# Two dense products of a spectral stage issued as pairs of 64 output columns

## The chip, the cores and the metric

The kernel runs on one core of one Trainium2 chip. The metric is the device time in microseconds (us). A core has TensorE (PE, which multiplies matrices; the loading of its stationary operand is listed apart as PEld), VectorE (DVE), ScalarE (ACT), GpSimd (POOL) and SyncE (SP, which here issues DMAs). Each engine takes its instructions in the order of the program and waits for the others by semaphores.

## The reference

Two kinds of layer alternate, twice each, on one sequence of 2048 rows and 512 features. Layer A is a global filter in the frequency domain; layer B is a gated feed-forward layer without a nonlinearity.

```
def A(x, w_r, w_i):                 # x: 1 x 2048 x 512
    X = rfft2(x, axes=(-2, -1))
    return irfft2(X * (w_r + 1j * w_i), s=(2048, 512), axes=(-2, -1))

def B(x, w_gate, w_up, w_down):     # 512 -> 1792 -> 512
    return ((x @ w_gate) * (x @ w_up)) @ w_down

x = x + A(layernorm(x), A_w_r, A_w_i)
x = x + B(layernorm(x), B_w_gate, B_w_up, B_w_down)
x = x + A(layernorm(x), A_w_r, A_w_i)
x = x + B(layernorm(x), B_w_gate, B_w_up, B_w_down)
```

## The kernel before

The two-dimensional transforms are done as products with small constant matrices. A spectral layer has three stages. The forward stage takes the 16 row tiles of x one after the other (a product `tp` on TensorE each) and writes a spectrum `E`. The middle stage, which the change touches, works on 16 groups g of `E`. The inverse stage (`yi`, then `yo`) needs all 16 groups, and adds the result to `xs`, the residual stream. Then comes the feed-forward layer (`gx`, `gy`, `gw`, `gz`, `gv`, and `db` or `ex`, `ey`, `ew`, `ez`, `ev`), most of the run.

A group g goes through the middle stage in this way, one 128 x 512 tile in each step:

1. `fs`: sums and differences of halves of `E`, two instructions on POOL (on DVE for the first two groups).
2. `dp` (function `features` in `middles`): eight products of 64 output columns on PE. The stationary operand is 64 columns of `fs`, the moving one a 128 x 128 block of the constant `df`. They write partitions 0 to 63 and 64 to 127 of a PSUM bank in turn.
3. `zs`: ACT copies `dp` to SBUF.
4. `zp` (function `across` in `middle`): one product on PE with a constant 128 x 128 matrix from `midt` as the stationary operand, and all 512 columns of `zs` as the moving one. Group 0 has two products of 256 columns with two different matrices.
5. The complex filter `W` (tile `wq`), in one of two ways by turns. Way "1": ACT copies the two halves of `zp` into `jz`, DVE multiplies `zp`, POOL multiplies `jz`, DVE adds them to `ys`. Way "2": four instructions on DVE, which write `ys` and `qp`.
6. `vq` (function `back`): four products on PE with 128 x 128 blocks of `ys` as the stationary operand and a matrix from `midt` as the moving one.
7. `E`: ACT copies `vq` back into its place in `E`.

All products here are float32. Each is seen in the profile as two matmul records, its two passes, each with a weight load.

What stands where is not left to a scheduler: every step is recorded in a `Plan`, and a table of numbers, `ORDER`, gives the order in which the steps are issued; a second one, `PLACES`, gives each tile its buffer. Neither table is touched by the change. In this order PE takes several groups in turn, so that a `dp` of later groups stands between `zp` and `vq` of earlier ones. In each layer `dp` stands in 8 runs, of 24, six times 16, and 8 products. The product `wp`, which belongs to no result, is placed by the helper `idle` before the stage and after its last `vq`.

The kernel keeps eight banks of 128 x 512 in PSUM: `dp`, `zp` and `vq` take turns in those tagged x, a, d and w, and a product that writes a bank also waits for the last reader of what was in it.

Since a helper (line 314 in the profile) issues every recorded instruction, all rows of the profile carry that one line, and are told apart by the names of their tiles.

Of the kernel before, what the change touches and what calls it, by code (L numbers as in the profile page):

```python
# [283 lines left out]
def kernel(ctx: ExitStack, tc: tile.TileContext, x, wf, wc, wb, dfwd, tf, ti, mid, out):  # L284
# [8 lines left out]
    def bank(name, tag):  # L293
        t = Tile_(name, tag, lambda: pp.tile([128, 512], F32, name=name, tag=t.tag(), bufs=1))
        return t

    def temp(name, tag, shape=(128, 512), dt=F32):
        t = Tile_(name, tag, lambda: wk.tile(list(shape), dt, name=name, tag=t.tag(), bufs=1))
        return t
# [20 lines left out]
    V, A, G, TE, SP = (Queue(e) for e in (nc.vector, nc.scalar, nc.gpsimd, nc.tensor, nc.sync))  # L320
# [3 lines left out]
    def mm3(o, sh, sl, mh, ml, start, stop):  # L324
        for n, (a, b) in enumerate(((sh, mh), (sh, ml), (sl, mh))):
            TE.matmul(o, a, b, start=start and n == 0, stop=stop and n == 2, skip_group_check=True)

    def dve(n, fn, r, w, **kw):
        return plan.op("DVE", max(0.12, 0.07 + 0.00104 * n), 0.155 + 0.00104 * n, fn, r, w, **kw)

    def act(n, fn, r, w, more=0.0, **kw):
        return plan.op("ACT", 0.05 + 0.00086 * n + more, 0.16 + 0.00084 * n + more, fn, r, w, **kw)

    def pool(n, fn, r, w, **kw):
        return plan.op("POOL", 0.15 + 0.00215 * n, 0.2 + 0.0021 * n, fn, r, w, **kw)

    def pe(us, fn, r, w, **kw):
        return plan.op("PE", us, us, fn, r, w, **kw)
# [18 lines left out]
    f2, f20, g2, g20 = (midt[:, 128 * i:128 * i + 128] for i in range(4))  # L357
# [20 lines left out]
    def load_hp():  # L378
        load(32, lambda: SP.dma_start(hp, wc), (), ["hp"])
        dve(32, lambda: V.tensor_scalar(hp[:, 1], hp[:, 1], -1.0, None, op0=ALU.mult), ["hp"], ["hp"], due=HPDUE)  # L380
# [24 lines left out]
    def stats(t, nm, on_act=False):  # L405
        i = nm.ts.index(t)
        if on_act:
            z = temp("sq", "f")
            a = temp("ac", "st", (128, 6))
            act(512, lambda: A.activation(z(), xs[:, t], AF.Copy, accum_out=a()[:, 0:1]), [("xs", t)], [z, (a, 0)], more=0.25)  # L410
            act(20, lambda: A.mul(a()[:, 1:2], a()[:, 0:1], -1.0 / 512), [(a, 0)], [(a, 1)])
            act(512, lambda: A.activation(z(), xs[:, t], AF.Square, bias=a()[:, 1:2], accum_out=a()[:, 2:3]),
                [("xs", t), (a, 1)], [z, (a, 2)], more=0.25)
            dve(10, lambda: V.tensor_scalar(nm.mv()[:, i, 0:1], a()[:, 0:1], 1.0 / 512, None, op0=ALU.mult), [(a, 0)], [(nm.mv, i)])
            dve(10, lambda: V.tensor_scalar(nm.mv()[:, i, 1:2], a()[:, 2:3], 1.0 / 512, None, op0=ALU.mult), [(a, 2)], [(nm.mv, i)])
            return
        st = temp("st", "st", (128, 6))
        dve(512, lambda: V.bn_stats(st(), xs[:, t]), [("xs", t)], [st])
        dve(20, lambda: V.bn_aggr(nm.mv()[:, i], st()), [st], [(nm.mv, i)])
# [104 lines left out]
    def idle(n, key="idle", ring="w", cols=512):  # L524
        for i in range(n):
            bk = bank("wp", ring)
            pe(cols / 595, lambda bk=bk: TE.matmul(bk()[:, 0:cols], midt[:, 0:128], midt[:, 0:cols], start=True, stop=True), ["midt"], [bk, key])
# [29 lines left out]
    def middle(g, dp, E, W, due, swap):  # L557
        zs = temp("zs", "f")
        act(512, lambda: A.copy(zs(), dp()), [dp], [zs])
        zp = bank("zp", "da"[g % 2])  # L560

        def across():
            if g:
                TE.matmul(zp(), f2, zs(), start=True, stop=True)
            else:
                for q, m in enumerate((f20, f2)):
                    TE.matmul(zp()[:, 256 * q:256 * q + 256], m, zs()[:, 256 * q:256 * q + 256], start=True, stop=True, skip_group_check=True)

        pe(0.86, across, [zs, "midt"], [zp])
        y, w = temp("ys", "f"), W.key[g // 2]  # L570
        if swap == "1":
            jz = temp("jz", "f")
            act(512, lambda: A.mul(jz()[0:64], zp()[64:128], -1.0), [zp], [(jz, 0)], more=0.11)
            act(512, lambda: A.copy(jz()[64:128], zp()[0:64]), [zp], [(jz, 1)], more=0.11)
            dve(512, lambda: tt(zp(), zp(), W(g, 0), ALU.mult), [(jz, 0), (jz, 1), w], [zp])
            pool(512, lambda: gtt(jz(), jz(), W(g, 1), ALU.mult), [w], [(jz, 0), (jz, 1)])
            dve(512, lambda: tt(y(), zp(), jz(), ALU.add), [zp, (jz, 0), (jz, 1)], [y])
        else:
            qp = bank("qp", "y")
            dve(512, lambda: tt(y(), zp(), W(g, 0), ALU.mult), [zp, w], [y])  # L580
            dve(512, lambda: stt(qp()[0:64], zp()[64:128], -1.0, W(g, 1)[64:128], op0=ALU.mult, op1=ALU.mult), [zp, w], [(qp, 0)])
            dve(512, lambda: tt(qp()[64:128], zp()[0:64], W(g, 1)[0:64], ALU.mult), [zp, w], [(qp, 1)])
            dve(512, lambda: tt(y(), qp(), y(), ALU.add), [(qp, 0), (qp, 1)], [y])
        vq = bank("vq", "wd"[g % 2])

        def back():
            for q in range(2):
                for par in range(2):
                    o = 256 * q + 128 * par
                    TE.matmul(vq()[:, o:o + 128], y()[:, o:o + 128], g2 if g or q else g20, start=True, stop=True, skip_group_check=True)  # L590

        pe(0.92, back, [y, "midt"], [vq, *(["turn"] if g > 14 else [])])
        if g > 14:
            idle(1, "turn", "a")
        into = lambda: E()[:, :, :, g].rearrange("p b t (q e) -> p q (b t) e", q=2)
        act(512, lambda: A.copy(into(), vq().rearrange("p (q c e) -> p q c e", q=2, e=4)), [vq], [(E, "g", g, 0), (E, "g", g, 1)], more=0.11, due=due)
# [590 lines left out]
```

## Time and profile before

| | before |
|---|---|
| median of 3 runs | 1048.96 us (1048.85 to 1051.21) |
| profiled execution, first to last instruction (span) | 1048.2 us |
| instructions | 18805 |
| PE busy | 1032.4 us, 6560 matmul records |
| `dp` | 512 records of 128x128, stationary 128 x 64 |
| `zp` | 60 records of 128x512, 8 of 128x256, stationary 128 x 128 |
| `vq` | 256 records of 128x128, stationary 128 x 128 |
| granted PE clock | 1.000 |
| middle stage of layer 0 | 28.2 to 75.4 us of the span |
| middle stage of layer 1 | 548.1 to 594.0 us of the span |

The page has no other time of the profiled execution than its span; it is 0.8 us below the median. A row of the timeline reads: start and length in us, engine, line, operation, tile written and tiles read, for a matmul the array in use (`128*64` is 128 rows and 64 columns of the array), the shape, the number of merged records, and in square brackets how long the engine stood idle before it and which engine ended that. The ends of matmuls are modelled and rows of PE overlap, so the distance between two starts tells what a product costs, and not its length. Busy times of the engines overlap.

### The profile page before, as it was taken

Reading aid. Unit: us, or ns where it says so; the run is one execution under the profiler, and the core shown is the slowest. Engines: PE = TensorE matmul, PEld = TensorE weight load, DVE = VectorE, ACT = ScalarE, POOL = GpSimd, SP = SyncE. Lnnn points to the kernel's source line nnn. Section 1 sums busy time; section 2 is a strip of 40 time slices with the busy share of each in tenths; the row PEclk is TensorE's granted clock in tenths of the full one; section 3 lists DMA queues with packets and bytes.
Section 4 is the critical chain, followed back from the end, with each engine's and each line's share of the span. In section 5 each row is a group of like instructions: output and inputs, shape, how many; then the busy total and the mean of one; then the engine's idle time right before and its main releaser. Section 6 shows DMA issues by size and latency. Waiting matters only on the chain.

```text
span 1048.2 us, 18805 instructions
## 1 busy us (share of the span) xinstructions
PE 1032.4 (98%) x6560; PEld 900.8 (86%) x6560; DVE 803.6 (77%) x1581; ACT 421.0 (40%) x1011; POOL 747.0 (71%) x960
## 2 busy tenths in 40 slices
PE   9899999999999999999999999999999999999998
PEld 7677988888899888889987779888889998888887
DVE  7769867768877577878877697788888775767788
ACT  6568534343453232232366693223333421222231
POOL 6968899999999645566688367555578963536671
PEclk9999999999999999999999999999999999999999
DMA  9525266668773864646382005455787266464542
GB/s 360 224 83 191 64 218 229 234 214 277 253 213 140 278 215 158 201 164 230 120 319 78 6 12 201 153 176 176 190 275 219 91 222 220 162 211 179 213 141 81
DMA packets 129469, 193.66 MB, mean 185 GB/s; under 512 B 39264, under 2 KB 50784, under 8 KB 127328
## 3 DMA queue, kind: packets, MB, share of 16 engines
q1 hardware_dynamic: 129088, 191.95, 54.1%
q8 instruction: 52, 0.85, 0.3%
q10 hardware_dynamic: 288, 0.52, 0.1%
q14 instruction: 41, 0.34, 0.1%
HBM read 145.52 MB, written 46.92 MB: 184 GB/s over the span
## 4 chain that ended last, share of the span: by engine, by line
PE 90%; DVE 6%; POOL 1%; ACT 1%; DMA 1%; issue 1%; SPq 0%; DVEq 0%; POOLq 0%; ACTq 0%
PE gz L314 15%; PE gx L314 15%; PE db L314 8%; PE gy L314 7%; PE gw L314 7%; PE gv L314 7%; PE ex L314 5%; PE ez L314 5%; PE ey L314 3%; PE dp L314 3%; PE ev L314 3%; PE vq L314 3%; PE ew L314 3%; PE zp L314 2%; DVE xs L314 2%; PE yi L314 2%
## 5 line engine op out<-in xcount | busy, mean ns | idle before, releaser
L314 PE MATMUL gx<-xA,wt 128*128 128x512 f32 (+1 forms) x852 | 179.3, 346 | 0.0
L314 PEld LDWEIGHTS gx<-xA,wt 128*128 128x128 f32 x852 | 137.9, 190 | 17.9
L314 POOL TENSOR_TENSOR sf<-q,sf 128x256 fp32r<-128x256 f32 x99 | 73.0, 742 | 106.4 <-ACT sf L314 97.3
L314 POOL TENSOR_TENSOR sf<-cc,sf 128x256 fp32r<-128x256 f32 x97 | 71.7, 742 | 55.8 <-ACT sf L314 48.9
L314 DVE TENSOR_TENSOR xs<-xs,db 128x512 f32<-128x512 f32 x128 | 85.5, 681 | 23.1 <-PE db L314 22.6
L314 PE MATMUL db<-wd,h 128*128 128x512 f32 x336 | 91.1, 392 | 0.1
L314 PE MATMUL gy<-xS,wt 128*128 128x512 f32 (+1 forms) x426 | 89.9, 346 | 0.0
L314 PE MATMUL gz<-xS,wt 128*128 128x512 f32 (+1 forms) x426 | 89.9, 346 | 0.0
L314 PE MATMUL gz<-xA,wt 128*128 128x512 f32 (+1 forms) x426 | 89.6, 346 | 0.0
L314 PE MATMUL gw<-xS,wt 128*128 128x512 f32 (+1 forms) x426 | 89.5, 346 | 0.0
L314 PE MATMUL gv<-xS,wt 128*128 128x512 f32 (+1 forms) x426 | 89.4, 345 | 0.0
L314 ACT COPY s<-gx 128x512 f32<-128x512 f32 (+1 forms) x71 | 35.2, 496 | 132.0 <-PE gx L314 131.7
L314 PEld LDWEIGHTS gz<-xS,wt 128*128 128x128 f32 x426 | 69.0, 189 | 9.5 <-DVE q L314 0.4
L314 PEld LDWEIGHTS gw<-xS,wt 128*128 128x128 f32 x426 | 69.1, 189 | 9.1
L314 PEld LDWEIGHTS gz<-xA,wt 128*128 128x128 f32 x426 | 69.0, 189 | 9.0
L314 PEld LDWEIGHTS gv<-xS,wt 128*128 128x128 f32 x426 | 69.0, 190 | 9.0
L314 PEld LDWEIGHTS gy<-xS,wt 128*128 128x128 f32 x426 | 68.6, 190 | 8.6
L314 DVE TENSOR_TENSOR q<-gy,s 128x512 f32<-128x512 f32 (+1 forms) x71 | 41.0, 577 | 45.2 <-PE gy L314 33.0
L314 ACT CAST sf<-q 128x256 fp32r<-128x256 f32 x99 | 40.0, 407 | 82.0 <-DVE q L314 41.5
L314 PEld LDWEIGHTS db<-wd,h 128*128 128x128 f32 x336 | 61.1, 188 | 11.6 <-POOL h L314 0.2
L314 POOL TENSOR_TENSOR wt<-rg,wt 128x512 fp32r<-128x512 f32 (+1 forms) x56 | 64.2, 1158 | 5.2 <-ACT wt L314 5.1
L314 PE MATMUL ex<-bf,sf 128*128 128x256 f32 x396 | 58.1, 283 | 0.0
(166 smaller groups left out, 2507.9 us busy)
## 6 DMA issues: line engine op xcount, KB each, us to landing
wt<-gu SPq DMA_DIRECT2D x36, 1024.0 KB, 6.8
wt<-gu SPq DMA_DIRECT2D x36, 768.0 KB, 6.7
bf<-dn SPq DMA_DIRECT2D x20, 1024.0 KB, 5.4
wq<-in_wf_dram SPq DMA_DIRECT2D x16, 1024.0 KB, 8.3
bf<-dn SPq DMA_DIRECT2D x20, 768.0 KB, 4.7
gu<-wt SPq DMA_DIRECT2D x14, 1024.0 KB, 5.9
gu<-wt SPq DMA_DIRECT2D x14, 768.0 KB, 5.4
rg<-in_wb_dram SPq DMA_DIRECT2D x14, 512.0 KB, 3.9
```

Of the source, the lines that this page charges most:

```text
L314: ins = f(*args, **kw)
```

## The change

`zp` and `vq` are issued as pairs: a new helper `halves` takes columns 0 to 63 of the stationary operand into partitions 0 to 63 of the result, and then columns 64 to 127 into partitions 64 to 127, each with the whole moving operand. `dp` was issued in this form already. What is computed is the same. No step is moved, added or taken out, and no other engine has another instruction; only the numbers in the names of tiles differ.

```
+    def halves(o, a, b):
+        for c in (slice(0, 64), slice(64, 128)):
+            TE.matmul(o[c], a[:, c], b, start=True, stop=True, skip_group_check=True)
...
         def across():
             if g:
-                TE.matmul(zp(), f2, zs(), start=True, stop=True)
+                halves(zp(), f2, zs())
             else:
                 for q, m in enumerate((f20, f2)):
-                    TE.matmul(zp()[:, 256 * q:256 * q + 256], m, zs()[:, 256 * q:256 * q + 256], start=True, stop=True, skip_group_check=True)
+                    halves(zp()[:, 256 * q:256 * q + 256], m, zs()[:, 256 * q:256 * q + 256])
...
                     o = 256 * q + 128 * par
-                    TE.matmul(vq()[:, o:o + 128], y()[:, o:o + 128], g2 if g or q else g20, start=True, stop=True, skip_group_check=True)
+                    halves(vq()[:, o:o + 128], y()[:, o:o + 128], g2 if g or q else g20)
```

PE's order in the middle of layer 0's stage (the rows from 49.58 to 59.88 us of the profile before) was this; in these rows a shape is columns of the stationary operand by columns of the moving one, and a count is products:

```order
L314 MATMUL dp<-df,fs 64x128 x16
L314 MATMUL zp<-zs,midt 128x512
L314 MATMUL vq<-midt,ys 128x128 x4
L314 MATMUL zp<-zs,midt 128x512
L314 MATMUL vq<-midt,ys 128x128 x4
L314 MATMUL dp<-df,fs 64x128 x16
```

The same place after the change:

```order
L314 MATMUL dp<-df,fs 64x128 x16
L314 MATMUL zp<-zs,midt 64x512 x2
L314 MATMUL vq<-midt,ys 64x128 x8
L314 MATMUL zp<-zs,midt 64x512 x2
L314 MATMUL vq<-midt,ys 64x128 x8
L314 MATMUL dp<-df,fs 64x128 x16
```

The rows stand in the same places, with twice the products of half the columns, and now every row has 64 columns. The end of the same stage on PE, before, with the numbers of the tiles:

```order
L314 MATMUL zp_874<-zs_870,midt_67 128x512
L314 MATMUL dp_880<-df_140,fs_786 64x128 x8
L314 MATMUL vq_893<-midt_67,ys_878 128x128 x4
L314 MATMUL vq_904<-midt_67,ys_579 128x128 x4
L314 MATMUL zp_912<-zs_901,midt_67 128x512
L314 MATMUL vq_916<-midt_67,ys_737 128x128 x4
L314 MATMUL vq_928<-midt_67,ys_899 128x128 x4
L314 MATMUL vq_936<-midt_67,ys_863 128x128 x4
L314 MATMUL vq_945<-midt_67,ys_922 128x128 x4
L314 MATMUL vq_956<-midt_67,ys_925 128x128 x4
L314 MATMUL wp_966<-midt_67 128x512
L314 MATMUL yi_974<-di_797,E_132 128x128 x4
```

And after (the numbers of tiles differ, the products they name are the same):

```order
L314 MATMUL zp_925<-zs_921,midt_67 64x512 x2
L314 MATMUL dp_932<-df_140,fs_822 64x128 x8
L314 MATMUL vq_945<-midt_67,ys_930 64x128 x8
L314 MATMUL vq_960<-midt_67,ys_583 64x128 x8
L314 MATMUL zp_972<-zs_957,midt_67 64x512 x2
L314 MATMUL vq_977<-midt_67,ys_767 64x128 x8
L314 MATMUL vq_993<-midt_67,ys_955 64x128 x8
L314 MATMUL vq_1005<-midt_67,ys_910 64x128 x8
L314 MATMUL vq_1018<-midt_67,ys_987 64x128 x8
L314 MATMUL vq_1033<-midt_67,ys_990 64x128 x8
L314 MATMUL wp_1047<-midt_67 128x512
L314 MATMUL yi_1055<-di_837,E_132 128x128 x4
```

The change from 64 to 128 columns, which stood behind `dp_880` before, now stands behind the last `vq`, ahead of `wp`. The last rows of DVE in that stage, before; they are the same after the change but for the numbers:

```order
L314 TENSOR_TENSOR zp_874<-zp_874,wq_134 128x512
L314 SCALAR_TENSOR_TENSOR qp_891<-zp_858,wq_125 64x512
L314 TENSOR_TENSOR ys_899<-qp_891,ys_899 128x512
L314 TENSOR_TENSOR ys_922<-zp_874,jz_889 128x512
L314 TENSOR_TENSOR ys_925<-zp_912,wq_134 128x512
L314 SCALAR_TENSOR_TENSOR qp_934<-zp_912,wq_134 64x512
L314 TENSOR_TENSOR qp_934<-zp_912,wq_134 64x512
L314 TENSOR_TENSOR ys_925<-qp_934,ys_925 128x512
```

Nothing moved here: the last `vq` of PE reads the `ys` that is DVE's last row, which comes from the last `zp`.

## The prediction

> **What bounds the kernel now.** I read the page first, then the busy time in the two stretches that the change touches, then TensorE's (PE's) own rows in order of time there, and last the rows of the engines that PE waits for. In the first fence are the page's busy line of PE and its chain of waits by engine; in the second the busy time of the two middle spectral stages (one for each layer).
>
> ```profile
> PE 1032.4 (98%) x6560; PEld 900.8 (86%) x6560; DVE 803.6 (77%) x1581; ACT 421.0 (40%) x1011; POOL 747.0 (71%) x960
> ...
> PE 90%; DVE 6%; POOL 1%; ACT 1%; DMA 1%; issue 1%; SPq 0%; DVEq 0%; POOLq 0%; ACTq 0%
> ```
>
> ```profile
> core 0: us, PE busy (x) PEld busy (x) DVE busy (x) ACT busy (x) POOL busy (x), PEclk, DMA share, GB/s
> 28.20:75.40 47.20, 46.09 (x420) 34.55 (x420) 33.37 (x50) 29.59 (x54) 38.72 (x52) 1.00 0.36 135
> 548.10:594.00 45.90, 45.86 (x420) 34.71 (x420) 32.93 (x49) 27.94 (x49) 29.21 (x39) 1.00 0.17 66
> ```
>
> PE is the bound, 98% of the span and 90% of the chain, and in the middle stages too (46.09 of 47.20 us, 45.86 of 45.90) at the full clock (1.00). But VectorE (DVE) is at 33 of 46 to 47 us there, and its work has holes and unbroken blocks; whether PE time that is saved reaches the end of the stage depends on those blocks. Next are PE's own rows (start, length, what, number of records).
>
> ```profile
> 49.58 1.97 PE L314 MATMUL dp<-df,fs 128*64 128x128 f32 x32
> 51.48 1.12 PE L314 MATMUL zp<-zs,midt 128*128 128x512 f32 x2
> 52.44 1.05 PE L314 MATMUL vq<-midt,ys 128*128 128x128 f32 x8
> 53.33 1.02 PE L314 MATMUL zp<-zs,midt 128*128 128x512 f32 x2
> 54.19 1.05 PE L314 MATMUL vq<-midt,ys 128*128 128x128 f32 x8
> 55.18 1.97 PE L314 MATMUL dp<-df,fs 128*64 128x128 f32 x32
> ...
> 66.35 1.10 PE L314 MATMUL dp<-df,fs 128*64 128x128 f32 x16
> 67.37 2.05 PE L314 MATMUL vq<-midt,ys 128*128 128x128 f32 x16
> ...
> 74.59 1.02 PE L314 MATMUL wp<-midt 128*128 128x512 f32 x2
> 75.45 0.80 PE L314 MATMUL yi<-di,E 128*128 128x128 f32 x5
> ```
>
> Each f32 product is two records (two passes). Lengths in these rows overlap, so I go by starts. A zp between two vq takes 54.19 - 53.33 = 0.86 us (0.43 a pass), a vq 53.33 - 52.44 = 0.89 (0.111 a record). A dp run of 32 records takes 51.48 - 49.58 = 1.90, one of 16 records 67.37 - 66.35 = 1.02: 16 records more cost 0.88, so 0.110 for every two. So two dp passes of 64 columns run side by side, in the time of one vq pass of 128. What is left of a dp run, 1.90 - 16 x 0.110 = 0.14, is a fixed charge. The neighbours carry more of it: the zp after dp takes 52.44 - 51.48 = 0.96, 0.10 over the undisturbed one, and the vq ahead of dp 55.18 - 54.19 = 0.99, 0.10 over 0.89. Together a dp run costs 0.34 to 0.35 us beside its arithmetic, wherever it stands between products of the other tiling. I put 0.15 at its entry (the late start, and 0.05 of its weight load laid bare) and 0.20 at its exit.
>
> **The change part by part.** *The switches.* Each layer has 8 dp runs among the zp and vq (24, six times 16, and 8 products). After the change all three share the tiling, and a change of tiling is left at the first entry (PE stands waiting there anyway) and at the last exit, which moves from dp to the end of the last vq. So 7 x 0.35 = 2.45 us of PE's time go in each layer.
>
> *The products themselves.* zp issues two products of 64 columns over the same 512 moving columns, vq eight of 64 over 128 in place of four. If halves pair as in dp, a zp stays at 0.86 and a vq comes to 8 x 0.109 = 0.87, 0.02 less: 16 x 0.02 = 0.3 a layer. The nearest row for pairing is the start of the first dp run, asked for with a window of 70 ns:
>
> ```profile
> 28.24 0.14 PEld L314 LDWEIGHTS dp<-df,fs 128*64 128x64 f32 x2 [2.58 <-DVE fs L314]
> 28.24 0.33 PE L314 MATMUL dp<-df,fs 128*64 128x128 f32 x2 [1.75 <-DVE fs L314]
> ```
>
> Two passes begin there at once, though the second product stands behind both passes of the first in program order. dp is written as halves now will be: partitions 0 to 63, then 64 to 127, in turn. No row shows a 64-column product over 512 columns; its price per zp lies between 0.86 (paired, as dp) and 1.72 (one after the other). I take 0.86, since dp is the nearest. The 128 more vq products and 34 more zp products need no time of their own, as dp issues at the same rate.
>
> So PE alone would be 2.45 + 0.3 = 2.75 us shorter in each layer. *What takes its place* are waits for DVE, which I follow block by block. Layer 0 first:
>
> ```profile
> 32.61 0.59 ACT L314 COPY zs<-dp 128x512 f32<-128x512 f32 x1
> 32.77 0.19 PEld L314 LDWEIGHTS zp<-zs,midt 128*128 128x128 f32 x1
> ...
> 37.01 0.70 DVE L314 TENSOR_TENSOR qp<-zp,wq 64x512 f32<-64x512 f32 x1 [1.04 <-PE zp L314]
> ...
> 44.38 1.86 PEld L314 LDWEIGHTS vq<-midt,ys 128*128 128x128 f32 x16 [0.24 <-DVE ys L314]
> ...
> 47.75 0.68 DVE L314 TENSOR_TENSOR ys<-qp,ys 128x512 f32<-128x512 f32 x1
> 48.49 1.16 PE L314 MATMUL vq<-midt,ys 128*128 128x128 f32 x8 [0.34 <-DVE ys L314]
> ...
> 59.56 0.70 DVE L314 TENSOR_TENSOR zp<-zp,wq 128x512 f32<-128x512 f32 x1 [2.94 <-ACT jz L314]
> ...
> 67.67 0.70 DVE L314 TENSOR_TENSOR zp<-zp,wq 128x512 f32<-128x512 f32 x1 [0.18 <-ACT jz L314]
> ...
> 72.52 0.69 DVE L314 TENSOR_TENSOR ys<-qp,ys 128x512 f32<-128x512 f32 x1
> 74.79 0.58 ACT L314 COPY E<-vq 128x512 f32<-128x512 f32 x1 [0.31 <-PE vq L314]
> ```
>
> DVE's block from 37.01 began on a zp of PE's. By then PE has gained the first exit (0.20, of which about 0.1 is lost, as the second zp's weights wait for ScalarE's (ACT's) copy and load at 32.77), an entry (0.15) and an exit (0.20): 0.46. The block has no holes until after 52, so it moves 0.46. PE waits for it at 44.38 and 48.49 (its ys ends at 47.75 + 0.68), so of the 1.2 us that PE has gained by then only about 0.5 is left. From there it gains the entry at 49.58, the exit at 51.48, an entry at 55.18 and two vq: 0.5 + 0.15 + 0.20 + 0.15 + 0.04, 1.05 in all. The block from 59.56 began on ACT's jz, which follows that dp and the zp after it: it moves 1.05. Its only hole to the end is the 0.18 at 67.67, on a jz that moves further; 0.15 of it closes. So the last ys, which ended at 72.52 + 0.69 = 73.21, ends at 72.01. The last vq of the layer began at 74.59 - 0.89 = 73.70; now it waits until 72.01 + 0.05 + 0.06 (a signal and a bare weight load, the steps of 48.43 to 48.49 and of the dp entry) = 72.12. That is 1.58 earlier. Now comes the new exit ahead of wp, 0.20; yi waits for wp and for ACT's copy of the last vq too (74.79 + 0.58 = 75.37), behind which its weights still load, so about half of the 0.20 is covered. Layer 0: 1.58 - 0.10 = 1.48. Layer 1 the same way:
>
> ```profile
> 562.90 1.28 POOL L314 TENSOR_TENSOR jz<-jz,wq 128x512 f32<-128x512 f32 x1
> 567.04 1.27 POOL L314 TENSOR_TENSOR jz<-jz,wq 128x512 f32<-128x512 f32 x1
> ...
> 564.21 0.69 DVE L314 TENSOR_TENSOR ys<-zp,jz 128x512 f32<-128x512 f32 x1
> 569.10 0.68 DVE L314 TENSOR_TENSOR ys<-zp,jz 128x512 f32<-128x512 f32 x1
> 570.11 0.69 DVE L314 TENSOR_TENSOR ys<-zp,wq 128x512 f32<-128x512 f32 x1 [0.33 <-PE zp L314]
> ...
> 575.81 0.69 DVE L314 TENSOR_TENSOR ys<-zp,jz 128x512 f32<-128x512 f32 x1
> 576.55 0.30 PEld L314 LDWEIGHTS zp<-zs,midt 128*128 128x128 f32 x2 [0.82 <-DVE ys L314]
> ...
> 583.68 0.70 DVE L314 TENSOR_TENSOR zp<-zp,wq 128x512 f32<-128x512 f32 x1 [1.25 <-ACT jz L314]
> ...
> 591.18 0.69 DVE L314 TENSOR_TENSOR ys<-qp,ys 128x512 f32<-128x512 f32 x1
> 593.21 1.02 PE L314 MATMUL wp<-midt 128*128 128x512 f32 x2
> ```
>
> Here GpSimd (POOL) holds first: its rows carry no idle time before them, since it works through fs without a break, and the ys at 564.21 starts as jz ends (562.90 + 1.28). It cannot move. The ys at 569.10 needs the jz that ends at 568.31, and moves 0.7 at most. So DVE's block from 570.11, whose zp PE would bring 1.55 earlier, moves 0.7 and its own hole of 0.33: 1.0 to 1.1. PE's zp at 576.55 waits for that block's ys (575.81 + 0.69), and 1.1 is what PE keeps. Then an entry, an exit and two vq, 0.39, give 1.49 at the zp whose jz starts the block of 583.68; that block has no hole to 591.18 + 0.69 = 591.87, and ends at 590.38. The last vq began at 593.21 - 0.89 = 592.32, now at 590.38 + 0.11 = 590.49: 1.83, less 0.10 at the exit. Layer 1: 1.7.
>
> *The sum*: 1.48 + 1.7 = 3.2 us. The profiled execution spans 1048.2, and 1045.0 is left; the median of the three runs is 0.76 above that span (1048.96), so I forecast 1045.8. It carries on to the end, because the stage's end is a meeting point: behind yi all start anew, as DVE does:
>
> ```profile
> 77.08 1.65 DVE L314 TENSOR_TENSOR vs<-yi,yb 128x256 f32<-128x256 f32 x4 [3.87 <-ACT yb L314]
> ```
>
> **The rivals.** *DVE holds more.* If its blocks hardly moved (POOL's jz, as in layer 1, or a bank that comes free late), each layer would keep only the slack of its last vq: 73.70 - 73.21 - 0.11 = 0.38 and 592.32 - 591.87 - 0.11 = 0.34, less 0.1 each: 0.5 us, 1048.4. Between that and the forecast, 1047.3. For it speaks that I followed few of the waits; against it, that the holes at 59.56 (2.94) and 583.68 (1.25) end on work that PE starts.
>
> *All of it comes through.* 2 x (2.75 - 0.10) = 5.3, 1043.7. The waits at 48.49 and 576.55, there already, speak against it.
>
> *The passes keep their written order.* If the second half could start only after the first half's second pass had started, a zp would take three pass times, 1.29 in place of 0.86, and its last pass could share the array with no more than the next product's first. That is 0.2 to 0.43 for each of 32 zp, 6.4 to 13.8 us lost against 3.2 gained: slower from 0.1 us a zp on, and about 1056. Against it stand the two passes at 28.24 and the x16 run: it would need nine pair times, 0.99 beside its charge of 0.14, and has 1.02 in all. The Trainium skill (TensorE: Matmul & The Clock Gate, Part 3, The mechanism) says this very thing: matmuls start and end strictly in program order, with no reordering. By that rule the sum would be 1056; the rows of dp do not agree with it.
>
> *No pairing over 512 columns.* Every zp 0.86 longer: 32 x 0.86 = 27.5, some 1073. Nothing in the trace speaks for it but that no such row exists.
>
> *The charge is not the tiling's.* If it came with each change of operands, it would stay, and the time with it (1049). Against it: zp to vq and vq to zp change operands too and carry none (0.86 and 0.89).
>
> **How the numbers follow.** The forecast, 1045.8 with 1044.9 to 1046.8 of its own, has 0.64; DVE holding more (1046.8 to 1048.6) 0.16; all through 0.08; written order 0.06; no pairing 0.03; no effect 0.03. The range leaves out the last three and all through: 1044.4 to 1048.4. 0.3% is 3.15 us, about what a measurement of this kernel tells from no change, and the forecast lies just on it: half of its weight and all through make faster 0.42; the other half, DVE and no effect, same 0.49; slower 0.09.
>
> **What would show it.** In the changed profile: zp as x4 records of 128*64 in 0.86 us between vq, vq x16 in 0.87; dp runs of 32 at 1.75 from start to start of the next, without the 0.10 on their neighbours; a gap of 0.2 ahead of wp; longer waits of vq for DVE's ys at some 44, 48 and 72 us, and of a zp at some 575; yi at about 74.0 (75.45 before). If zp takes over 1 us, the pairing is wrong; if yi comes at 72.8, DVE's blocks gave more than I think; if later waits swallow the 1.5 us, the meeting point is wrong.

## Result, and the profile after

The changed kernel takes 1047.67 us (median of 8 runs, 1046.15 to 1047.90), the kernel before 1050.22 us (8 runs, 1048.85 to 1051.21; the three known at the time of the prediction are among them and had a median of 1048.96). The ratio is 0.9973, with a 95% interval of 0.9964 to 0.9983: 2.6 us less. That is a real gain, and just under the 0.3% that the prediction took as the line between faster and same. The forecast was 1045.8 in a range of 1044.4 to 1048.4; the time lies in the range, 1.9 us above the forecast, and outside the 1044.9 to 1046.8 that the prediction gave to its own mechanism.

From the page of the profiled execution of the changed kernel, PE's busy line and the chain of waits by engine:

```profile
PE 1028.3 (98%) x6884; PEld 898.9 (86%) x6884; DVE 803.7 (77%) x1581; ACT 421.3 (40%) x1011; POOL 748.4 (72%) x960
...
PE 86%; DVE 5%; POOL 4%; issue 1%; ACT 0%; DVEq 0%; POOLq 0%; ACTq 0%
```

PE is 4.1 us less busy (1032.4 before) with 324 records more, and its part of the chain fell from 90% to 86%, while POOL's rose from 1% to 4%: other engines now end some of the time. PE's rows in the middle of layer 0's stage, in order of time:

```profile
52.38 1.03 PE L314 MATMUL zp<-zs,midt 128*64 128x512 f32 x4
53.23 1.04 PE L314 MATMUL vq<-midt,ys 128*64 128x128 f32 x16
54.11 1.03 PE L314 MATMUL zp<-zs,midt 128*64 128x512 f32 x4
54.97 1.04 PE L314 MATMUL vq<-midt,ys 128*64 128x128 f32 x16
55.84 1.92 PE L314 MATMUL dp<-df,fs 128*64 128x128 f32 x32
57.59 1.03 PE L314 MATMUL zp<-zs,midt 128*64 128x512 f32 x4
```

By starts, a `zp` takes 54.97 - 54.11 = 0.86 us, a `vq` 0.87 to 0.88, and a `dp` run 57.59 - 55.84 = 1.75 (1.90 before). The neighbours of `dp` carry nothing: the `zp` ahead of the second `vq` takes the same 0.86 as any other. So the halves pair, over 512 columns too, and the charge at the change of tiling is gone. The waits of PE that grew are these (kind, total, times, longest); before, the first was 0.3 us in all and the second was not listed:

```profile
PE vq L314 <- DVE ys L314: 1.0, 2, 0.5
PE zp L314 <- DVE ys L314: 0.9, 1, 0.9
```

They stand at the products where the prediction has them (in layer 0 some 1.5 us later than it says, for the reason below):

```profile
45.60 1.97 PE L314 MATMUL vq<-midt,ys 128*64 128x128 f32 x32 [0.53 <-DVE ys L314]
...
49.70 1.09 PE L314 MATMUL vq<-midt,ys 128*64 128x128 f32 x16 [0.42 <-DVE ys L314]
...
575.85 1.08 PE L314 MATMUL zp<-zs,midt 128*64 128x512 f32 x4 [0.91 <-DVE ys L314]
```

I measure the stage from the start of its first `dp` to the start of the first `yi`. Before, that was 28.24 to 75.45 (47.21 us) in layer 0 and 548.14 to 594.07 (45.93 us) in layer 1. In the profile after (length, busy time of PE, PEld, DVE, ACT and POOL, then the granted clock):

```profile
28.55:75.81 47.26, 45.37 (x583) 34.65 (x584) 33.31 (x50) 29.70 (x54) 38.80 (x52) 0.96 0.36 135
548.50:592.87 44.37, 43.46 (x582) 33.26 (x583) 32.87 (x49) 27.71 (x49) 29.31 (x39) 1.00 0.18 68
```

Layer 1 is 1.56 us shorter. Layer 0 has gained nothing, and its granted clock is 0.96 where it was 1.00. PE's rows there, and the clock in steps of 1 us (the third number from the end):

```profile
30.37 3.34 PE L314 MATMUL dp<-df,fs 128*64 128x128 f32 x32 [0.72 <-DVE fs L314]
33.53 1.99 PE L314 MATMUL zp<-zs,midt 128*64 128x256 f32 x12
```

```profile
29.00:30.00 1.00, 0.65 (x12) 0.41 (x8) 1.00 (x2) 0.00 (x0) 1.00 (x3) 0.90 1.08 434
30.00:31.00 1.00, 0.63 (x6) 0.66 (x8) 0.22 (x1) 0.59 (x1) 1.00 (x2) 0.50 1.05 438
...
32.00:33.00 1.00, 1.00 (x14) 1.00 (x12) 0.00 (x0) 0.00 (x0) 1.00 (x3) 0.50 0.95 401
33.00:34.00 1.00, 1.00 (x16) 0.88 (x15) 0.00 (x0) 0.20 (x1) 1.00 (x2) 0.89 1.04 434
```

One run of 16 `dp` products takes 33.53 - 30.37 = 3.16 us, since PE had half its clock from about 29.8 to 33.2 us. So about 1.4 us of layer 0's gain (47.26 against 45.89 in a profile without that stretch, shown below) is given back to something that was in none of the prediction's cases. In this kernel six of the eight runs had a mean granted clock of 0.997 or 0.998 (1047.5 to 1047.9 us), and two had 0.999 (1046.2); times of one kernel therefore have two levels here, and I compare stages only between profiles without that stretch.

### The profile page after: what moved, and what is told of

It is laid out like the page before. It is cut to its first block, busy times and chain, and to the rows that moved or that the text cites. A ratio compares the mean times of both kernels' runs of the same rounds, so it can differ in the third digit from the quotient of the medians.

```text
span 1046.0 us, 19456 instructions
## 1 busy us (share of the span) xinstructions
PE 1028.3 (98%) x6884; PEld 898.9 (86%) x6884; DVE 803.7 (77%) x1581; ACT 421.3 (40%) x1011; POOL 748.4 (72%) x960
## 4 chain that ended last, share of the span: by engine, by line
PE 86%; DVE 5%; POOL 4%; issue 1%; ACT 0%; DVEq 0%; POOLq 0%; ACTq 0%
PE gz L314 15%; PE gx L314 15%; PE db L314 8%; PE gy L314 7%; PE gw L314 7%; PE gv L314 7%; PE ex L314 5%; PE ez L314 5%; PE ey L314 3%; PE ew L314 3%; PE ev L314 3%; DVE xs L314 2%; PE vq L314 2%; POOL fs L314 2%; PE yi L314 2%; PE dp L314 1%
```

## Experiments

**The stretch at half clock.** PE stood idle for 1.75 us ahead of the first `dp` of layer 0's stage. Three `wp` products in place of one fill that wait:

```
-    def idle(n, key="idle", ring="w", cols=512):
+    def idle(n, key="idle", ring="w", cols=512, times=1):
+        def keep(bk):
+            for _ in range(times):
+                TE.matmul(bk()[:, 0:cols], midt[:, 0:128], midt[:, 0:cols], start=True, stop=True)
...
-            pe(cols / 595, lambda bk=bk: TE.matmul(bk()[:, 0:cols], midt[:, 0:128], midt[:, 0:cols], start=True, stop=True), ["midt"], [bk, key])
+            pe(cols / 595, lambda bk=bk: keep(bk), ["midt"], [bk, key])
...
-        idle(IDLE[layer])
+        idle(IDLE[layer], times=1 if layer else 3)
```

In the kernel before:

> The kernel before, with three wp products in place of one ahead of layer 0's middle spectral stage (each 0.86 us; TensorE waited 1.75 us there), so that TensorE stands idle for almost nothing ahead of the first dp. Theory (the clock's stretch at 0.50 that the changed kernel's profile shows from 29 to 33 us comes from the low activity around that wait, and is what lifts four of eight runs of before to 1050.9): all runs at clock 1.000 and at 1048.9, 0.9987 of the kernel before. Rival (the stretch has another cause, or is none of before's two levels): two levels as before, 1048.9 and 1050.9, and no change of the mean.

In the changed kernel:

> The changed kernel with the same three wp products ahead of layer 0's stage. Theory: the stretch at clock 0.50 goes, all runs are at the level of the two best of the changed kernel, 1046.2 (0.9973 to 0.9975 of the kernel before with three wp products, 2.6 to 2.8 us less), and the profile has PEclk 1.00 from 28 to 36 us and layer 0's stage shorter by about 1.4 us than in the changed kernel's profile. Rival (the first dp runs long for another reason, say the transfers beside it): the dp run at 30.4 us still takes over 3 us, and the time stays at 1047.7.

And the changed kernel once more, unaltered, with later runs:

> The changed kernel itself, unaltered, beside the others on the same chip. Theory (most of its runs hold a stretch at clock 0.50 in layer 0's stage, worth 1.4 us): two levels, 1046.2 and 1047.7, and a median nearer the upper; the one with three wp products was at 1046.3 in all its runs. Rival (the two levels came from the chip or the hour): all runs at 1046.3.

The kernel before with three `wp` took 1049.45 us (11 runs; ratio to the kernel before 0.9991, 0.9982 to 1.0000), the changed kernel with three 1046.32 us (5 runs; 0.9963, 0.9949 to 0.9976), and the changed kernel alone 1046.35 us (5 runs, of which the one at clock 0.998 took 1047.58; 0.9969, 0.9956 to 0.9981). On this chip only one of its five runs had a clock under 0.999, not most of them as expected. Where the clock of each run is listed, 21 of 71 runs of the kernel before and 7 of 13 of the changed kernel (six of these seven in its first eight runs) had a mean clock of 0.998 or less; of the 97 runs of kernels with three `wp`, none. So filling the wait removes the stretch, in both kernels. That it comes from the low activity of PE at that place is the plain reading; of the kernel before, only the mean clocks tell of it, and no profile shows it. Not all of the spread goes with the clock: the kernel before with three `wp` came to 1049.45 and not to the 1048.9 expected, and one of its runs took 1051.36 at a mean clock of 1.000, for a reason that no run here shows. The stages of the two kernels with three `wp`, that before first (length, PE busy, clock; layer 0 and layer 1):

```profile
28.30:75.50 47.20, 46.14 (x420) 1.00 0.36 135
548.32:594.24 45.92, 45.92 (x420) 1.00 0.18 67
```

```profile
28.16:74.05 45.89, 44.00 (x582) 1.00 0.38 142
546.70:591.07 44.37, 43.46 (x582) 1.00 0.18 71
```

The change is worth 1.31 us in layer 0 and 1.55 in layer 1, 2.86 together; the medians say 3.13. The unaltered changed kernel, in a profile without the stretch, has the same stages (74.38 - 28.49 = 45.89 and 591.44 - 547.06 = 44.38):

```profile
28.49 1.10 PE L314 MATMUL dp<-df,fs 128*64 128x128 f32 x16 [1.75 <-DVE fs L314]
...
74.38 2.84 PE L314 MATMUL yi<-di,E 128*128 128x128 f32 x24
...
547.06 2.93 PE L314 MATMUL dp<-df,fs 128*64 128x128 f32 x48 [0.64 <-DVE fs L314]
...
591.44 3.73 PE L314 MATMUL yi<-di,E 128*128 128x128 f32 x32
```

The changed kernel with three `wp` took 1046.32 us, and the changed kernel alone the same 1046.35 on another chip, where the stretch was rare: what the two more products bring is steadiness.

**One product alone in halves.** If the gain is the switch, half of the change must make the kernel slower than before, since there are then more switches and not fewer. Both kernels have three `wp`. `zp` alone, with `vq` as before:

```
-                    halves(vq()[:, o:o + 128], y()[:, o:o + 128], g2 if g or q else g20)
+                    TE.matmul(vq()[:, o:o + 128], y()[:, o:o + 128], g2 if g or q else g20, start=True, stop=True, skip_group_check=True)
```

> zp in halves of 64 columns, vq whole as before, with the three wp products. Theory (the gain is the switch between the two array tilings, 0.35 us for each stretch of narrow products): the narrow stretches of a layer are 10 in place of 8 before and 1 in the changed kernel, so 4 x 0.35 = 1.4 us SLOWER than the kernel before with three wp products, about 1050.3. Rival (halves are cheaper in themselves, each part brings its share): some 1.4 us faster, 1047.5.

`vq` alone, with `zp` as before:

```
-                halves(zp(), f2, zs())
+                TE.matmul(zp(), f2, zs(), start=True, stop=True)
...
-                    halves(zp()[:, 256 * q:256 * q + 256], m, zs()[:, 256 * q:256 * q + 256])
+                    TE.matmul(zp()[:, 256 * q:256 * q + 256], m, zs()[:, 256 * q:256 * q + 256], start=True, stop=True, skip_group_check=True)
```

> vq in halves, zp whole as before, with the three wp products. Theory (switches at 0.35 us): narrow stretches 14 in layer 0 and 10 in layer 1 in place of 8 and 8, 8 x 0.35 = 2.8 us more, less 0.6 for vq's own shorter halves: 2.2 us SLOWER than the kernel before with three wp products, about 1051.1. Rival (halves are cheaper in themselves): 1 to 2 us faster, about 1047.5.

They took 1050.40 us (11 runs, 1049.94 to 1051.42) and 1051.19 us (11 runs, 1050.72 to 1052.62), against 1049.45 for the kernel before with three `wp` on the same chip: 0.95 and 1.74 us slower. Their ratios to the kernel before, without the three `wp`, are 1.0003 (0.9994 to 1.0012) and 1.0013 (1.0005 to 1.0022). The rival, that each part brings its share, would have made both about 0.2% faster, and is out. The two stages together, first of `zp` alone, then of `vq` alone:

```profile
sum 94.19, PE 93.11; mean PE 46.55
```

```profile
sum 94.84, PE 93.94; mean PE 46.97
```

Against the 93.12 (47.20 + 45.92) of the kernel before with three `wp`, that is 1.07 and 1.72 us, some three quarters of the 1.4 and 2.2 that 0.35 us a switch gives. Either a switch is cheaper away from `dp`, or waits for DVE that were there before cover part of it.

**DVE relieved.** Both kernels have three `wp`, and compute only the first 128 of 512 columns of the three operations on `qp` in way "2" (the rest of that part of the filter is left out), so that each of these takes DVE 0.30 us in place of 0.70, some 1.2 us less for every second group:

```
-            dve(512, lambda: stt(qp()[0:64], zp()[64:128], -1.0, W(g, 1)[64:128], op0=ALU.mult, op1=ALU.mult), [zp, w], [(qp, 0)])
...
+            k = slice(0, 128)
+            dve(512, lambda: stt(qp()[0:64, k], zp()[64:128, k], -1.0, W(g, 1)[64:128, k], op0=ALU.mult, op1=ALU.mult), [zp, w], [(qp, 0)])
...
-            dve(512, lambda: tt(y(), qp(), y(), ALU.add), [(qp, 0), (qp, 1)], [y])
+            dve(512, lambda: tt(y()[:, k], qp()[:, k], y()[:, k], ALU.add), [(qp, 0), (qp, 1)], [y])
```

> The kernel before with three wp products, and VectorE relieved: of the three operations on qp in every second group only the first 128 of 512 columns are computed (the rest of that part of the filter is left out). Theory (TensorE is the bound of both stages and waits there 0.3 us for VectorE's ys): 0.3 to 0.6 us less than without the relief, about 1049.0. Rival (VectorE bounds the stages of before too): over 2 us less.

> The changed kernel with three wp products and the same relief of VectorE. Theory (VectorE's blocks keep back the part of TensorE's saving that does not come through: TensorE's busy time fell 4.6 us in the two stages, the stages only 2.9): the waits for ys go, the two stages become 4.0 to 4.6 us shorter than those of the kernel before with the relief, and the time is some 1044.6. Rival (something else holds, ScalarE's zs or GpSimd's jz): the difference stays at 2.9 us, 1046.0.

The kernel before with the relief took 1048.57 us (11 runs), the changed kernel with it 1042.84 us (5 runs; ratio to the kernel before 0.9933, 0.9920 to 0.9945). The stages of the first and of the second:

```profile
28.86:75.39 46.53, 45.81 (x421) 1.00 0.35 133
548.25:593.92 45.67, 45.67 (x421) 1.00 0.18 68
```

```profile
27.97:71.81 43.84, 43.11 (x583) 1.00 0.40 149
544.48:587.46 42.98, 42.98 (x583) 1.00 0.18 69
```

By itself the relief takes 0.92 us from the two stages of the kernel before (93.12 to 92.20): more than the 0.3 to 0.6 expected, and far from the 2 us of its rival. The change is now worth 2.69 us in each layer, 5.38 in all, and PE's waits for `ys` are gone from the list. So DVE held back 5.38 - 2.86 = 2.5 us of what PE saved. My expectation of 4.0 to 4.6 was too low: I took PE's busy time for the price of its work (92.06 - 87.46 = 4.6), and busy time, with modelled ends that overlap, is not that. The prediction's own count of 2.75 less 0.10 a layer was the better one.

With the same relief, the kernels with one product alone in halves show whether a switch has one price:

> zp alone in halves, with three wp products and VectorE relieved as in the two relieved kernels (the same part of the filter is left out), so that TensorE's own price is seen. Theory (a switch of tilings costs 0.35 us whatever the neighbours): two switches more in each layer than the kernel before with the same relief, 4 x 0.35 = 1.4 us more in the two stages together (92.2 there, 93.6 here), 1050.0. Rival (a switch between zp and vq costs less than one at a dp run, as the 0.95 to 1.1 us without the relief has it, 0.25 each): 1.0 us more, 1049.6.

> vq alone in halves, with three wp products and the same relief. Theory: six switches more in layer 0 and two in layer 1, 8 x 0.35 = 2.8 us, less 0.6 for vq's own halves: 2.2 us more in the two stages (94.4), 1050.8. Rival (0.25 a switch): 1.4 more, 1050.0.

They took 1049.92 and 1050.62 us (10 runs each). Their two stages together, `zp` alone first:

```profile
sum 93.71, PE 92.97; mean PE 46.49
```

```profile
sum 94.32, PE 93.60; mean PE 46.80
```

Against 92.20 that is 1.51 us for four switches (0.38 each) and 2.12 for eight, less 0.6 (0.34 each). A switch costs about the same beside `dp` and between `zp` and `vq`; the quarter that was missing without the relief had been covered by waits. The rows of `zp` alone show it:

```profile
51.70 1.16 PE L314 MATMUL vq<-midt,ys 128*128 128x128 f32 x8
52.79 1.08 PE L314 MATMUL zp<-zs,midt 128*64 128x512 f32 x4
53.80 1.16 PE L314 MATMUL vq<-midt,ys 128*128 128x128 f32 x8
```

A `vq` now takes 52.79 - 51.70 = 1.09 in place of 0.89, and a `zp` 53.80 - 52.79 = 1.01 in place of 0.86: 0.20 and 0.15 on each pair.

**The order of the halves.** Is it the order by turns that pairs them? `vq`'s halves by fours (three `wp`, without the relief):

```
-            for q in range(2):
-                for par in range(2):
-                    o = 256 * q + 128 * par
-                    halves(vq()[:, o:o + 128], y()[:, o:o + 128], g2 if g or q else g20)
+            for c in (slice(0, 64), slice(64, 128)):
+                for q in range(2):
+                    for par in range(2):
+                        o = 256 * q + 128 * par
+                        TE.matmul(vq()[c, o:o + 128], y()[:, o:o + 128][:, c], g2 if g or q else g20, start=True, stop=True, skip_group_check=True)
```

> The changed kernel with three wp products, and vq's eight half products in another order: the four of partitions 0 to 63 first, then the four of 64 to 127, in place of by turns. The same products, the same tiling. Theory (a product shares the array only with the product right behind it on the other half, so the order by turns is what pairs them): seven of eight pair times stand one after the other, 4 x 0.22 + 3 x 0.22 = 1.54 us for a vq in place of 0.87, 32 x 0.67 = 21 us of TensorE's time more, less some 2 that it waits now: about 1065. Rival (TensorE reads far enough ahead to feed both halves whatever the order): vq x16 in 0.87, and 1046.3 as with turns.

It took 1049.56 us (11 runs; 0.9994, 0.9985 to 1.0003): 3.2 more than by turns (1046.32), neither the 19 of the theory nor the 0 of the rival. Its two stages together:

```profile
sum 93.71, PE 92.89; mean PE 46.44
```

That is 3.45 more than the 90.26 by turns. The same order with the relief, and by twos (the loop over c inside that over q):

> The changed kernel with three wp products and the same relief, and vq's halves by fours, as in the kernel with that order without the relief. Theory (the order costs 0.1 us where other products stand between two vq and 0.2 where vq follow one another, and without the relief some 2 us of it were covered by waits for VectorE): 32 x 0.15 = 5 us more than the changed kernel with the relief, 1047.8. Rival (nothing was covered, the 3.2 us seen without the relief are all): 1046.0.

> The changed kernel with three wp products and the same relief, and vq's halves by twos: two products of partitions 0 to 63, then two of 64 to 127, and again. Theory (each half of the array is fed by itself, with a look ahead of a few products, as the interleaved rows of the kernel with fours show): vq x16 stays near 0.87, the time within 1 us of the changed kernel with the relief, 1042.8 to 1043.8. Rival (each change from one half to the other costs what it did with fours): two changes in a vq cost 0.11 to 0.21 us there, four cost 0.2 to 0.4, 32 vq 7 us and more: 1050.

By fours it took 1047.23 us (8 runs), by twos 1043.24 (4 runs). PE's rows by fours, with the relief, show what happens:

```profile
52.31 1.20 PE L314 MATMUL vq<-midt,ys 128*64 128x128 f32 x13
53.25 0.33 PE L314 MATMUL dp<-df,fs 128*64 128x128 f32 x1
53.35 0.27 PE L314 MATMUL vq<-midt,ys 128*64 128x128 f32 x1
53.41 0.27 PE L314 MATMUL dp<-df,fs 128*64 128x128 f32 x1
53.46 0.27 PE L314 MATMUL vq<-midt,ys 128*64 128x128 f32 x1
```

Passes of the next `dp` run stand between the last passes of `vq`: PE feeds one half of the array with later products while the other half still works through earlier ones. How far ahead it goes must be limited, since by fours some time is lost all the same. The stages of both, by fours and then by twos:

```profile
sum 91.25, PE 90.53; mean PE 45.26
```

```profile
sum 86.92, PE 86.19; mean PE 43.09
```

By turns they were 86.82. So fours cost 4.43 us, 0.14 for each of 32 `vq`, of which waits for DVE covered 1.0 without the relief; and twos cost 0.1 us in all, which is nothing.

## Why the prediction was right, and where it was off

*The charge of a switch.* 0.34 to 0.35 us per `dp` run was read from the starts of neighbouring rows in one profile. With DVE out of the way seven switches and `vq`'s own 0.3 are worth 2.69 us a layer, where the prediction has 2.75 less 0.10; half changes priced a switch at 0.34 and 0.38. The charge is shown, and its size nearly so: since the new exit takes 0.2 to 0.25 and not 0.10 (below), the seven switches come to some 0.37 each, and the two small errors cancel.

*Pairing.* 0.86 and 0.87 as forecast. That the first two passes of a `dp` run start together at 28.24 was enough to choose rightly between the rivals. "The passes keep their written order" would have made a `zp` 1.29 and did not come; "no pairing over 512 columns" neither. The rule of the Trainium skill (TensorE: Matmul & The Clock Gate, Part 3, The mechanism) that matmuls start and end strictly in program order does not hold for the starts in the two halves of the array here: at 53.25, in the kernel by fours, a pass of `dp` starts ahead of passes of `vq` that were written before it.

*DVE's blocks.* The prediction has the last `vq` of a layer wait for DVE until 43.88 us (72.12 - 28.24) after the first `dp` in layer 0, and 42.35 (590.49 - 548.14) in layer 1. The changed kernel with three `wp` has, among the weight loads (PEld):

```profile
72.03 0.88 PEld L314 LDWEIGHTS vq<-midt,ys 128*64 128x64 f32 x16 [0.30 <-ACT wd L314]
73.09 0.30 PEld L314 LDWEIGHTS wp<-midt 128*128 128x128 f32 x2 [0.17 <-issue]
...
589.05 0.88 PEld L314 LDWEIGHTS vq<-midt,ys 128*64 128x64 f32 x16 [0.17 <-ACT E L314]
```

The weights of that `vq` load 72.03 - 28.16 = 43.87 and 589.05 - 546.70 = 42.35 us after the first `dp`, a few hundredths ahead of the product itself. The ACT named in layer 0 is the cast of a weight tile of the feed-forward layer, which has no part in this product; DVE's last `ys` ends at 71.23 + 0.69 = 71.92, just before:

```profile
71.23 0.69 DVE L314 TENSOR_TENSOR ys<-qp,ys 128x512 f32<-128x512 f32 x1
```

In layer 1 DVE's last `ys` (588.25 + 0.69) and the copy of `E` named there both end at 588.94, so that row alone does not tell which of the two it was. The steps on the way came out too. The rows that the prediction has at 37.01, 59.56, 570.11 and 583.68 are now

```profile
36.48 0.70 DVE L314 TENSOR_TENSOR qp<-zp,wq 64x512 f32<-64x512 f32 x1 [0.69 <-POOL jz L314]
58.42 0.70 DVE L314 TENSOR_TENSOR zp<-zp,wq 128x512 f32<-128x512 f32 x1 [2.72 <-ACT jz L314]
...
567.61 0.68 DVE L314 TENSOR_TENSOR ys<-zp,wq 128x512 f32<-128x512 f32 x1
580.74 0.70 DVE L314 TENSOR_TENSOR zp<-zp,wq 128x512 f32<-128x512 f32 x1 [0.86 <-ACT jz L314]
```

Counted from the first `dp` of their layer they moved 0.45, 1.06, 1.06 and 1.50 us, where the prediction has 0.46, 1.05, 1.0 to 1.1 and 1.49. Following DVE's blocks by their holes gave both ends within 0.1 us. The relief shows the same from the other side: held back were 2.5 us.

*The exit.* This term was mis-sized. The prediction lets the 0.20 us of the new exit ahead of `wp` be half covered by ACT's copy of the last `vq`. From the load of its weights the last `vq` needs 73.09 - 72.03 = 1.06 to `wp`'s own bare load, and `wp` 74.05 - 73.09 = 0.96 to `yi`, 2.02 in all; in layer 1 the same steps run from 589.05 to 591.07, 2.02 again. Before, they took 75.45 - 73.70 = 1.75 in the prediction's own working, from the start of the product. So the exit costs 0.2 to 0.25 us, and nothing of it is covered. The prediction's own rows had no room for cover: `yi` came 75.45 - 74.59 = 0.86 after `wp`, the bare price of `wp`, so whatever delays `wp` delays `yi`. With a few hundredths by which the last `vq` begins later than forecast, about 0.15 more is lost in each layer: 1.31 in place of 1.48, 1.55 in place of 1.7, and 2.86 in place of 3.2.

*The clock, and luck.* The other 1.5 us between the forecast and the median are the stretch at half clock, which the prediction did not look for, since the profile before shows 1.00 throughout. That the median still lies in the stated range is luck: 1047.67 falls in the part that was kept for "DVE holds more" (1046.8 to 1048.6), and that is not what happened. The runs of the changed kernel without the stretch have a median of 1046.2, inside the forecast's own 1044.9 to 1046.8. The stretch lifts the kernel before as well, though less often, so the base of 1048.96, from three runs, was low beside the 1050.22 of eight. (The 0.76 us that the prediction adds to the span is no property of the kernel. Every run whose span is listed took 1.7 to 1.9 us more than its span, so the 0.76 sets the span of one run against the time of another; it drops out, as the forecast is 1048.96 less 3.2.) By medians over all runs whose clock is listed, the change is worth the same at either level: 1046.2 against 1049.7 us for runs of a mean clock of 0.999 or more, 1047.7 against 1051.1 for the others. These were not all on one chip; the 3.13 us between the two kernels with three `wp`, which were, is the better figure.

*The rivals.* "DVE holds more" did not come: 1.31 and 1.55 are far from 0.3. "All of it comes through" is what the relieved kernels do, 5.38 us where it has 5.3, so it named the right price under the condition that failed. The chances of faster and same were about even (its own weights add up to 0.40 and 0.51, where it has 0.42 and 0.49), and the ratio fell 0.03% on the side of same.

## What to carry to other kernels

Where products of 64 columns stand among products of 128, bring all of a stage to one tiling or leave them alone: one at a time adds switches and is slower. Price such a switch from starts of neighbouring rows (0.35 us here), and then follow the engine behind, block by block, to see how much of it can come through; half of it did not, until that engine was relieved. Halves may stand by turns or by twos, but not by fours.

## What the runs showed of the hardware

A wait of 1.75 us, between a `wp` product and a `dp` run with gaps, was enough to halve the granted clock, though not in every run: the profile before has the same wait at 28.24, and a later one of the changed kernel at 28.49, both without the stretch. The rows of the profile after sum to 0.10 + 3 x 0.50 + 0.11 = 1.71 us of clock lost, or 3.42 us at half clock. The Trainium skill (TensorE: Matmul & The Clock Gate, Part 1) has half rate and a window of about 3.4 us, which agrees; it has the throttle follow a window that was idle, and here PE was busy for 0.80 + 1.10 us of the four from 26 to 30:

```profile
26.00:28.00 2.00, 0.80 (x2) 1.00 1.00 418
28.00:30.00 2.00, 1.10 (x16) 0.95 1.04 424
```

Why it strikes some runs and not others was not tried. The Trainium skill (TensorE: Matmul & The Clock Gate, Part 1) has that window free-running, so that the time of a change of clock depends on where in the window the work falls; no run here shows it.

Not expected either: the two halves of the array are fed apart, with some look ahead (the interleaved rows by fours, where `dp` starts at 53.25 while `vq` goes on to 53.57), and a change of tiling costs about the same, 0.34 to 0.38 us in and out, whichever of the three kinds of product stand on its two sides.
